# Strided heads: the products with the values issued four quarters in turn

## The chip, the cores and the metric

One core of a Trainium2 chip runs the whole program. The metric is device microseconds (us) of one execution. TensorE (PE, with its weight loads shown as PEld) does the matrix products, VectorE (DVE) and ScalarE (ACT) the element-wise work, SyncE (SP) issues most transfers, and GpSimd (POOL) does almost nothing here.

## The reference

An attention over 4 batches, 8 heads, 576 positions and head size 64 is followed by two gated feed-forward blocks (model size 512, inner size 1024). Four heads are local (each position looks back over 32 positions), four are strided:

```python
mask_strided = (rel >= 0) & (pos[None, :] % stride == pos[:, None] % stride)
...
scores = np.where(masks[None, :, :, :], scores, -1000000000.0)
scores = scores - np.max(scores, axis=-1, keepdims=True)
attn = np.exp(scores)
attn = attn / (np.sum(attn, axis=-1, keepdims=True) + 1e-09)
return np.matmul(attn, v).astype(np.float32)
```

In a strided head only positions of one residue modulo 32 see each other, so the 576 positions fall into 32 classes of 18. The change touches only the last product of these heads, attention weights by values.

## The kernel before, in words

**Strided heads.** The kernel sorts positions by residue and takes three residues together: a block of 3 x 18 = 54 positions (SQ), 11 blocks a head. A pair of heads (ab = 0 and 1) of one batch is handled in two halves of 6 and 5 blocks (SB): one call of `unit` (lines 422 to 580) each, 16 such units in all (4 batches, 2 pairs, 2 halves). A unit makes the scores (line 467), masks them with a maximum on DVE (line 483), takes exponentials on ACT (line 488), normalises on DVE (line 499), turns two blocks at a time on PE (line 522) and copies the result into the tile `pt` (turned_out, lines 527 to 533). Even blocks then lie in rows 0 to 53 of `pt`, odd blocks in rows 64 to 117; the values `vt` lie in the same rows.

**The values' products.** `values` (lines 540 to 553) multiplies, for each block and each of the two heads, 54 rows of values by 54 rows of turned weights. The rows choose the upper or lower half of PE's array and the head the left or right half, so every product occupies one quarter of the array: an even block the two upper quarters, an odd block the two lower ones. Even blocks write the PSUM bank `pv`, odd blocks the bank `tr` in which the turned weights had stood. Each float32 product appears in the trace as two weight loads and two matmuls ("passes"), all on one line, so a unit of 6 blocks has 24 passes and one of 5 blocks 20. Before the change the kernel issues all even blocks, then all odd ones. `place` (lines 561 to 578) copies both banks to the tile xT.

**The strided scores** (line 467) have the same form, 64 rows by 64 columns with 54 columns moving, and the loop there goes over blocks so that four products in a row fall on four different quarters.

**What sets the order.** Everything up to the second feed-forward block is put into a planner (class Plan, lines 73 to 226) as jobs with estimated costs per engine; it lists them by the time at which they can start and by rank, and the instructions are issued on each engine in that order. The cost of a values job stands in line 555; other costs are fixed numbers as well, and PE's change between quarter and whole-array work is counted as 0.09. Up to 60 us of planned time the kernel also issues idle bf16 matmuls (`stir`, line 816) into PE gaps that the plan foresees (lines 863 to 868). Products of the first feed-forward block (line 649, `products`) fill PE between attention jobs. The second block (lines 907 and 975) has a plan of its own.

Of the kernel before, what the change touches and what calls it, by code (L numbers as in the profile page):

```python
# [23 lines left out]
SQ, SR, SB = 3 * NI, 118, (6, 5)  # L24
# [205 lines left out]
def block_kernel(ctx, tc, qkL, qkS, vL, vS, mu_k, mu_r, w_k, w_v, w_r, w_in, conv_w, w_out, ident, mask_l, mask_s, out):  # L230
# [29 lines left out]
    plan = Plan()  # L260
    fixed = {}

    def space(pool_, name, shape, dtype=F32, tag=None, bufs=1, parts=1):
        tag = tag or name
        return Space(tag, bufs, lambda: (pool_() if callable(pool_) else pool_).tile(shape, dtype, name=name, tag=tag, bufs=bufs), parts)
# [156 lines left out]
    def unit(b, p, half, loaded):  # L422

        qk, vts = loaded
        vt = vts[half]
        local = p < 2
        nb, nq, nk, rows = (LB[half], LQ, LK, P) if local else (SB[half], SQ, SQ, SR)
# [11 lines left out]
        n0 = (nb + 1) // 2  # L439
# [19 lines left out]
        pt = space(at, "pt", [P, LB[0] * P], bufs=2, parts=2)  # L459
# [78 lines left out]
        outs_ = [out_] if local else [out_, turned]  # L538

        def values(e):  # L540
            if local:
                for j in range(nb):
                    for ab in range(2):
                        r, o = slice(64 * ab, 64 * ab + 64), pos[j] * P + 64 * (ab ^ turn_of[j])
                        pe.matmul(out_()[r, j * nq:(j + 1) * nq], vt()[:nk, j, r], pt()[:nk, o:o + nq], start=True, stop=True)  # L545
                return

            for odd in range(2):
                rows = slice(64 * odd, 64 * odd + SQ)
                for i in range((nb - odd + 1) // 2):  # L550
                    for ab in range(2):
                        r, o = slice(64 * ab, 64 * ab + 64), i * SR + 64 * (ab ^ (odd and turn_of[1]))
                        pe.matmul(outs_[odd]()[r, i * nq:(i + 1) * nq], vt()[rows, 3 * half + i, r], pt()[rows, o:o + nq], start=True, stop=True)  # L553

        plan.add({"PE": nb * (0.146 if local else 0.105)}, values, [vt, pt], outs_)
        x, n = xT[b], nb * nq
        if local:
            copy(lambda: x()[:, p, 1 + first * nq:1 + (first + nb) * nq], lambda: out_()[:, :n], n, [out_], [(x, 2 * p + half)])
# [23 lines left out]
    def attention(b):  # L582
        xT[b] = space(wx, f"xT{b}", [P, KT, S + 1], tag="xT", bufs=2, parts=9)
        plan.add({"POOL": 0.1}, lambda e: pool.memset(xT[b]()[:, :, 0:1], 0.0), [], [(xT[b], 8)])
        for p in range(4):
            loaded = load(b, p)
            if b == 0 and p == 0:
                consts()
            for half in range(2):
                unit(b, p, half, loaded)  # L590
# [193 lines left out]
    for c in range(2, NCH):  # L784
# [17 lines left out]
        for m in (0, 2, 1, 3):  # L802
            group_v(c, m)
            if c >= 3 and later and (m % 2 or len(later) <= NF):
                f, i = later.pop()
# [75 lines left out]
    plan = Plan()  # L881
# [212 lines left out]
```

## Time and profile before

| | us |
|---|---|
| three runs, median (lowest to highest) | 530.18 (526.58 to 530.76) |
| the profiled execution, its own time | 528.08 |
| its span, first to last instruction | 526.3 |
| PE busy | 513.8 (98%) |
| DVE busy | 387.6 (74%) |
| ACT busy | 365.8 (70%) |
| passes of line 553 into `pv`, busy | 9.1 (192 passes) |
| passes of line 553 into `tr`, busy | 8.3 (160 passes) |

Busy time of PE counts a matmul from its start to its modelled end, and passes on different quarters overlap, so spacing of starts says more than busy time. The attention of the first batch lies in the first 35 us, that of the others in three stretches near 87 to 113, 168 to 197 and 244 to 268 us. The granted TensorE clock is full but for one stretch near 28 us.

### The profile page before, as it was taken

How to read it: one execution, taken by the hardware profiler on the slowest of the kernel's cores; microseconds unless marked ns; L12 is line 12 of the kernel's file. 1: busy time of each engine (PE TensorE's matmuls, PEld its weight loads, DVE VectorE, ACT ScalarE, POOL GpSimd, SP SyncE). 2: the span in 40 equal slices, each digit the busy share in tenths (PEclk: the TensorE clock that was granted, in tenths of full speed). 3: DMA queues.
4: the chain of work that ended last, by engine and by line, in shares of the span. 5: the costliest groups of instructions: out<-in, count | busy, mean ns of one | idle time of the engine just before them, and what ended most of it. 6: DMA issues, size and time to landing. Idle time of an engine off the chain costs nothing.

```text
span 526.3 us, 12014 instructions
## 1 busy us (share of the span) xinstructions
PE 513.8 (98%) x4470; PEld 476.7 (91%) x4470; DVE 387.6 (74%) x1125; ACT 365.8 (70%) x1086; POOL 1.6 (0%) x15
## 2 busy tenths in 40 slices
PE   7899999999999999999999999999999999999997
PEld 4679999899999899999999999989898989999885
DVE  4989999999956998955777414499996576677620
ACT  5999996999758999667989354475764454455420
POOL 0000000000000000000000000000000000000000
PEclk9989999999999999999999999999999999999999
DMA  7974566977566892771374440745127015401011
GB/s 221 337 236 151 168 195 200 369 233 245 190 209 211 284 352 100 258 272 50 122 254 185 139 141 1 284 148 203 41 72 283 22 40 181 176 20 41 20 42 60
DMA packets 50122, 88.87 MB, mean 169 GB/s; under 512 B 4240, under 2 KB 32528, under 8 KB 50064
## 3 DMA queue, kind: packets, MB, share of 16 engines
q1 hardware_dynamic: 49776, 87.95, 49.6%
q8 instruction: 35, 0.57, 0.5%
q14 instruction: 23, 0.19, 0.1%
q10 hardware_dynamic: 288, 0.16, 0.1%
HBM read 59.46 MB, written 28.64 MB: 167 GB/s over the span
## 4 chain that ended last, share of the span: by engine, by line
PE 75%; ACT 13%; DMA 5%; DVE 5%; issue 1%; ACTq 0%; DVEq 0%; SPq 0%
PE mm L649 37%; PE oo L975 18%; PE hh L907 14%; ACT pr L488 3%; ACT wb L299 2%; PE sc L467 2%; DMA x<-x_d 1%; DMA wi_d<-ws 1%; PE pv L545 1%; ACT mx L628 1%; PE pv L553 1%; DMA raw<-in_w_k 1%; DVE pr L483 1%; PE tr L522 1%; ACT rl L672 1%
## 5 line engine op out<-in xcount | busy, mean ns | idle before, releaser
L907 PEld LDWEIGHTS hh<-x,wi 128*128 128x128 f32 x672 | 94.8, 188 | 6.6 <-DVE hb L919 2.0
L907 PE MATMUL hh<-x,wi 128*128 128x288 f32 x672 | 98.5, 296 | 1.2 <-DVE hb L919 1.0
L649 PE MATMUL mm<-X,wvh 128*128 128x288 f32 x448 | 86.5, 301 | 0.0
L649 PEld LDWEIGHTS mm<-X,wvh 128*128 128x128 f32 x448 | 67.1, 188 | 1.0
L649 PE MATMUL mm<-Y,wkh 128*128 128x288 f32 x384 | 67.4, 294 | 0.0
L488 ACT ACTIVATE pr<-pr,nmx 128x54 f32<-128x54 f32 (+1 forms) x160 | 55.5, 358 | 5.8 <-DVE nmx L483 5.8
L649 PEld LDWEIGHTS mm<-Y,wkh 128*128 128x128 f32 x384 | 56.3, 188 | 0.1
L649 PE MATMUL mm<-Y,wrh 128*128 128x288 f32 x256 | 54.9, 302 | 0.5 <-ACT rs L661 0.5
L954 DVE SCALAR_TENSOR_TENSOR c<-hb,cw_sb,c 128x576 f32<-128x576 f32 x64 | 50.6, 812 | 0.0
L649 PE MATMUL mm<-X,wvl 128*128 128x288 f32 x224 | 47.9, 295 | 0.0
L690 DVE TENSOR_TENSOR X<-sq,X 128x288 fp32r<-128x288 f32 x48 | 21.9, 457 | 30.4 <-ACT X L688 24.6
L649 PEld LDWEIGHTS mm<-Y,wrh 128*128 128x128 f32 x256 | 42.4, 191 | 1.5 <-ACT rs L661 0.8
L975 PE MATMUL oo<-wo,gAh 128*128 128x512 f32 x160 | 43.4, 393 | 0.0
L649 PE MATMUL mm<-Y,wkl 128*128 128x288 f32 x192 | 40.9, 294 | 0.0
L649 PE MATMUL mm<-Y,wrl 128*128 128x288 f32 x128 | 38.3, 299 | 0.2 <-DVE wrl L350 0.2
L649 PEld LDWEIGHTS mm<-X,wvl 128*128 128x128 f32 x224 | 35.9, 188 | 0.0
L975 PE MATMUL oo<-wo,gBh 128*128 128x512 f32 x128 | 34.5, 392 | 0.0
L488 ACT ACTIVATION_READ_ACCUMULATOR pr<-pr,nmx 128x1 f32 x160 | 32.5, 203 | 0.0
L672 ACT ACTIVATE rl<-mm 128x288 f32<-128x288 f32 x64 | 26.6, 416 | 7.8 <-PE mm L649 7.6
L975 PEld LDWEIGHTS oo<-wo,gAh 128*128 128x128 f32 x160 | 28.1, 188 | 3.8
L649 PEld LDWEIGHTS mm<-Y,wkl 128*128 128x128 f32 x192 | 30.6, 188 | 0.0
L925 ACT ACTIVATE hb<-hb 128x288 f32<-128x288 f32 (+1 forms) x32 | 18.0, 564 | 15.4 <-DVE hb L919 15.3
(114 smaller groups left out, 1059.9 us busy)
## 6 DMA issues: line engine op xcount, KB each, us to landing
x_d<-xo SPq DMA_DIRECT2D x42, 288.0 KB, 3.9
x<-x_d SPq DMA_DIRECT2D x21, 576.0 KB, 4.9
wi_d<-ws SPq DMA_DIRECT2D x24, 256.0 KB, 4.3
wi<-wi_d SPq DMA_DIRECT2D x6, 896.0 KB, 6.3
qk<-in_qkS SPq DMA_DIRECT2D x8, 599.0 KB, 5.4
out<-ob SPq DMA_DIRECT2D x18, 256.0 KB, 2.0
qk<-in_qkL SPq DMA_DIRECT2D x7, 592.0 KB, 5.8
raw<-in_w_k SPq DMA_DIRECT2D x8, 512.0 KB, 3.7
```

Of the source, the lines that this page charges most:

```text
L299: act.activation(b(), hw, AF.Copy, scale=REBIAS)
L467: pe.matmul(bank_of[j]()[to:to + 64, at_[j]:at_[j] + nk], qk()[r, qo[j]:qo[j] + LQ], qk()[r, ko[j]:ko[j] + nk], start=True, stop=True)
L483: dve.tensor_tensor_reduce(pr()[:, i * gap:i * gap + nk], bank_of[i]()[:, at_[i]:at_[i] + nk], masks[i], -1.0 / 8.0, 3.0e38, ALU.add, ALU. ...
L488: act.activation(pr()[:, k], pr()[:, k], AF.Exp, bias=nmx()[:, i:i + 1], scale=-1.0, accum_out=sums()[:, i:i + 1])
L522: pe.transpose(turned()[:n, i // 2 * SR:(i // 2 + 1) * SR], pr()[:SR, i * gap:i * gap + n], id_sb[:SR, :SR])
L649: pe.matmul(o(), w_cols(name, j, t, part), x_[t](), start=(t == 0 and part == 0 and x_ is xhi), stop=(t == nk - 1 and x_ is xlo))
L672: plan.add({"ACT": 0.295}, lambda e: act.activation(r(), o(), AF.Relu), [o], [r])
L690: plan.add({"DVE": 0.37}, lambda e: dve.tensor_tensor(l_(), sq(), h_().bitcast(F32), ALU.subtract), [sq, h_], [l_])
L907: pe.matmul(o(), w(hw, j), x()[:, hx, j], start=anew and n == 0 and j == 0, stop=last and n == 2 and j == 1, skip_group_check=True)
L925: act.activation(h()[:, cols], h()[:, cols], AF.Relu)
L954: plan.add({"DVE": 0.735}, lambda e, k=k: dve.scalar_tensor_tensor(c(), h()[:, k:k + S], cw_sb[:, k * NF + f:k * NF + f + 1], c(), ALU.mul ...
L975: pe.matmul(o(), x_()[:, f, col:col + P], wsp["wo", f]()[:, part], start=(f == 0 and x_ is th and part == 0), stop=(f == NF - 1 and x_ is tl))
```

## The change

Inside `values`, the loop over pairs of blocks goes outside and the loop over even and odd inside, so that the products of one even and one odd block come one after the other. Operands, banks and the number of instructions are the same. The planner's cost of a strided values job goes from 0.105 to 0.07 for each block.

```diff
-            for odd in range(2):
-                rows = slice(64 * odd, 64 * odd + SQ)
-                for i in range((nb - odd + 1) // 2):
+            for i in range(n0):
+                for odd in range(min(2, nb - 2 * i)):
+                    rows = slice(64 * odd, 64 * odd + SQ)
                     for ab in range(2):
                         r, o = slice(64 * ab, 64 * ab + 64), i * SR + 64 * (ab ^ (odd and turn_of[1]))
                         pe.matmul(outs_[odd]()[r, i * nq:(i + 1) * nq], vt()[rows, 3 * half + i, r], pt()[rows, o:o + nq], start=True, stop=True)
 
-        plan.add({"PE": nb * (0.146 if local else 0.105)}, values, [vt, pt], outs_)
+        plan.add({"PE": nb * (0.146 if local else 0.07)}, values, [vt, pt], outs_)
```

## Rows read from the trace of the kernel before

**Rows 1.** Windows by stage: stretch, length, busy time (instructions) per engine, clock, DMA.

```profile
core 0: us, PE busy (x) PEld busy (x) DVE busy (x) ACT busy (x) POOL busy (x), PEclk, DMA share, GB/s
...
22.00:35.00 13.00, 11.53 (x182) 9.07 (x180) 11.67 (x51) 12.40 (x47) 0.00 (x0) 0.87 0.88 255
...
87.00:105.30 18.30, 17.96 (x306) 16.03 (x305) 17.25 (x95) 17.09 (x76) 0.00 (x0) 1.00 1.00 333
105.30:162.00 56.70, 56.67 (x515) 55.57 (x516) 46.70 (x137) 46.96 (x148) 0.10 (x1) 1.00 0.66 218
...
173.00:268.00 95.00, 95.00 (x1102) 90.47 (x1100) 75.01 (x284) 80.81 (x289) 0.00 (x0) 1.00 0.59 203
```

**Rows 2.** Waits of PE, 100 to 340 us: total us, times, longest.

```profile
PE pv L545 <- ACT xT L284: 1.0, 1, 1.0
PE pv L553 <- ACT xT L576: 0.4, 1, 0.4
```

**Rows 3.** Chain that ended last, near 28 us: start, us, what.

```profile
27.93 0.38 PE pv L553 x6
...
31.38 0.36 PE pv L553 x6
```

**Rows 4.** Line 553 over the span: ns min/median/max, first and last start.

```profile
L553 PE MATMUL pv<-pt,vt x192: 210/218/311, 23.2 to 267.7; 54*64 54x54 f32 x192
...
L553 PE MATMUL tr<-pt,vt x160: 218/218/348, 23.3 to 267.8; 54*64 54x54 f32 x160
```

**Rows 5.** PE's timeline, a 6-block values unit: start, us, instructions.

```profile
264.67 0.38 PE L553 MATMUL pv<-pt,vt 54*64 54x54 f32 x6
264.84 0.27 PE L553 MATMUL tr<-pt,vt 54*64 54x54 f32 x2
...
265.05 0.34 PE L553 MATMUL tr<-pt,vt 54*64 54x54 f32 x6
```

**Rows 6.** PE's timeline, a 5-block values unit and the product behind it.

```profile
267.38 0.38 PE L553 MATMUL pv<-pt,vt 54*64 54x54 f32 x6
...
267.76 0.22 PE L553 MATMUL tr<-pt,vt 54*64 54x54 f32 x2
267.92 0.40 PE L649 MATMUL mm<-Y,wrh 128*128 128x288 f32 x1
```

**Rows 7.** PE's timeline, strided scores of 6 and of 5 blocks.

```profile
247.13 0.57 PE L467 MATMUL sc<-qk 64*64 64x54 f32 x24
...
250.15 0.56 PE L467 MATMUL sc<-qk 64*64 64x54 f32 x20
```

**Rows 8.** PE's timeline, a 6-block values unit with local scores behind it.

```profile
188.56 0.38 PE L553 MATMUL pv<-pt,vt 54*64 54x54 f32 x6
...
189.12 0.51 PE L467 MATMUL sc<-qk 64*64 64x96 f32 x13
189.55 0.40 PE L649 MATMUL mm<-X,wvh 128*128 128x288 f32 x1
```

**Rows 9.** PE's timeline, local scores of 4 blocks between whole-array products.

```profile
244.19 0.56 PE L467 MATMUL sc<-qk 64*64 64x96 f32 x16
244.69 0.40 PE L649 MATMUL mm<-X,wvh 128*128 128x288 f32 x1
```

**Rows 10.** Windows around the low clock, columns as in rows 1.

```profile
24.80:28.20 3.40, 2.24 (x43) 1.44 (x42) 3.40 (x11) 3.40 (x13) 0.00 (x0) 0.98 1.01 280
28.20:31.60 3.40, 3.40 (x39) 3.02 (x41) 2.82 (x13) 3.17 (x13) 0.00 (x0) 0.52 0.57 162
```

**Rows 11.** PE's timeline, neighbouring products at the low and the full clock.

```profile
30.70 0.44 PE L649 MATMUL mm<-Y,wrl 128*128 128x288 f32 x1
30.94 0.44 PE L649 MATMUL mm<-Y,wrh 128*128 128x288 f32 x1
...
35.72 0.29 PE L649 MATMUL mm<-Y,wrl 128*128 128x288 f32 x1
35.85 0.43 PE L649 MATMUL mm<-Y,wrh 128*128 128x288 f32 x2
```

## The prediction

> **What bounds the kernel now.** I began with the windows by stage, because the average share of PE hides which stretches are its own. From 173 to 268 us PE is busy for all of the 95.00 us, and from 105.3 to 162 us for 56.67 of 56.70, at the full clock [rows 1]. There a shorter piece of PE work shortens the program. Earlier this doesn't hold: from 22 to 35 us ACT is busy for 12.40 of 13.00 us and PE for 11.53, and from 87 to 105.3 us PE still has gaps while DVE and ACT are above 17 of 18.3 us [rows 1]. Next I read the waits. After 100 us PE's attention jobs stood still twice in all: a local values job waited 1.0 us for ACT's copy to xT, and a strided values job 0.4 us for the copy of the unit before it, both for the single `pv` bank [rows 2]. The chain of waits then says which early values jobs matter: those that begin at 27.9 and 31.3 us are on it [rows 3]. Last I took the timeline of PE at single units, since the passes of line 553 last 0.218 us each but overlap [rows 4]; only first start, last end and the neighbours tell what a unit occupies.
>
> **What a values unit costs now.** A 6-block unit goes from 264.67 to 265.05 + 0.34 = 265.39: 0.72 us (rounding aside, 0.73). Its odd passes, in the bank `tr`, do not wait for the last even one: the first starts at 264.84, 0.17 us in, and from there the four quarters run together; but at the end six `tr` passes stand alone, with the upper half of the array empty [rows 5]. So PE already overtakes in part what the order of issue keeps apart, and only the rest can be won. A 5-block unit goes from 267.38 to 267.76 + 0.22, or 0.60 us (two more passes start a little later in that last row) [rows 6].
>
> **What it costs afterwards.** The nearest row is a close one: the strided scores run 64-column weights and 54 moving columns, with four quarters in turn, and take 0.57 us for 24 passes and 0.56 us for 20 [rows 7]. The 5-block unit has hardly less, since the two upper quarters still have six passes each, and the deepest quarter sets the end. Passes last 0.218 us in both. So a 6-block unit saves 0.73 - 0.57 = 0.16 us and a 5-block unit 0.60 - 0.56 = 0.04, which with the rounding I take as 0.05. The one difference is the order of the quarters: neighbours in the scores' order share no half, those in the new values' order share the upper or the lower one. But the even passes before the change, two quarters of one half, already run side by side [rows 5], so I expect no cost from it.
>
> A rule speaks against this. 23 steps between 24 starts take 0.57 - 0.22 = 0.35 us in the scores, about 15 ns a step [rows 4, 7]. The Trainium skill, "TensorE: Matmul & The Clock Gate", section "Wait — 56ns, not 53.3ns?", says that start-to-start never drops below about 25 ns however small the matmul is. An estimate by that page would be 23 x 25 = 575 ns, more than the 0.51 us between first and last start of today's unit, and so no gain at all. The trace disagrees for passes on different quarters, with 15 ns.
>
> **Where the values are followed by scores.** At 188.56 us the unit is followed by 16 passes of local scores, and they already fill the empty upper half: from the unit's start to the next whole-array product is 189.55 - 188.56 = 0.99 us [rows 8]. The same 16 passes alone take 244.69 - 244.19 = 0.50 [rows 9]. In the new order they can enter after 0.35 us plus one step of a quarter (six passes in 0.35, so about 0.06), which gives 0.91 us and saves 0.08; the upper bound is the whole 0.16. I take 0.10, nearer to the lower end because the cover is visible.
>
> **The sum.** Eight units have 6 blocks and eight have 5: 192 + 160 = 352 = 8 x 24 + 8 x 20 passes [rows 4]. Eleven start at 105.3 us or later, in stretches where PE sets the pace [rows 1].
> - Two 6-block units without scores behind them: 2 x 0.16 = 0.32.
> - Three 6-block units with scores behind them: 3 x 0.10 = 0.30.
> - Six 5-block units: 6 x 0.05 = 0.30.
> - The five early units (four in the first batch, one just ahead of the 0.4 us wait): 0 if ACT and DVE hide them all, 3 x 0.16 + 2 x 0.05 = 0.58 at most. The one ahead of the wait is hidden, since ACT is late there [rows 2]; two are on the chain [rows 3], 0.16 + 0.05. I take 0.2.
>
> That is 1.1 us, with 0 and 8 x 0.21 = 1.7 as bounds. Nothing is added: the number of instructions, transfers and banks is the same. No wait is new, since odd products write the bank `tr` only after turned_out has read it, and every values product needs turned_out's result anyway. `place` reads even blocks first; their last pass is late by one or two steps of 15 ns, the odd ones are early by 0.16. That copy is on ACT's or DVE's queue, with others ahead of it, and I count it as nothing.
>
> **The planner's cost** is the second half of the change, and its price can't be read from any row. The plan now counts 5 x 0.07 + 0.09 = 0.44 us for a 5-block unit, against 0.35 + 0.16 = 0.50 by rows (last start, then the step to the next product, [rows 6, 7]); before it was 5 x 0.105 + 0.09 = 0.62 against 0.54 from first pass to next product [rows 6]. Both are off by less than 0.1, so the plan isn't misled by much. But its later choices between jobs that are ready at nearly one time can flip from 23 us on. I bound this by what such choices cost today: the waits of 1.0 and 0.4 us could vanish or come again [rows 2], and so could the stretch at 28 us in which the granted clock is 0.52, the level of 1.2 GHz [rows 10]. There products start 0.24 us apart, against 0.13 at 2.4 GHz [rows 11]; in 3.4 us that loses 3.4 x (1 - 0.13 / 0.24) = 1.6 us of PE work. So about -3.0 to +3.0 us around the sum, and I take zero as the value, having no reason for a sign.
>
> **Against which time.** The profiled execution took 528.08 us (span 526.3 and 1.8 around it), so by its own time I get 527.0. It lies 2.1 below the median of the three runs, 530.18. Four executions are known, 526.58 to 530.76; the middle of them is (528.08 + 530.18) / 2 = 529.1, and 529.1 - 1.1 = 528.0 is my forecast. About 1%, 5.3 us, is what a measurement of this kernel can tell from no change, and the forecast lies well inside.
>
> **Rivals.**
> - **The order does nothing.** PE already runs odd passes ahead of the last even ones [rows 5]; if pairs in one half of the array hold each other up, two by two, the new order gives what the old one gave. For: the shared half is the one thing that the scores' rows don't have. Against: even passes of one half already start together. Time 529.1. The page's least step of 25 ns would end in the same time. Chance 0.10.
> - **Slower: the plan opens a new hole early.** Its place is the first 35 us, where PE has gaps and idle matmuls fill only those that the plan foresees. Before the low clock PE was busy for 2.24 of 3.40 us [rows 10]; a shorter values unit leaves it less busy still, and a second such stretch, on the path, costs 1.6. From one on it outweighs the 1.1: 529.1 - 1.1 + 1.6 = 529.6; with a new wait of 1.0 at the `pv` bank, 530.6. Against: the low stretch lies where ACT is nearly full, so part of it is hidden. Chance 0.22; over 1% needs four or five such events, 0.08.
> - **Faster by more: the new order closes the holes.** Without the two waits and the low stretch: 529.1 - 1.1 - 1.4 - 1.6 = 525.0. For: each of them hangs on a few tenths of a us of order. Against: the two later stretches have no hole to close. Chance 0.15.
> - The forecast itself has 0.53.
>
> **Range and chances.** The forecast's own range, with its bounds of 0 and 1.7 us and the spread of the known executions (2.1 to each side), is 525.5 to 530.5. With the two rivals on either side it reaches from 524.0 to 532.0, and leaves out about 2 in 10. Faster by over 1% (0.09) comes from the third rival with a low draw of runs, slower by over 1% (0.08) from the second; 0.83 is left for within 1%.
>
> **What would show it.** In the changed kernel's timeline a 6-block unit alternates two `pv` and two `tr` passes from the start, and lasts 0.57 us from first start to last end; a 5-block unit lasts 0.56. With scores behind it, first pass to next product falls from 0.99 to about 0.9. If units still last 0.72, the first rival holds. The windows from 105.3 us on should be shorter by 0.9 in all with PE as full as before. A second stretch at the low clock, or new lines among the waits of PE of 0.4 us or more, would show the planner's part to be larger than the products' own; then the forecast is wrong by that part, whichever way it goes.

## The result, and the profile after

The changed kernel takes 524.72 us (median of 6 runs, 523.68 to 525.66) against 529.38 us before in the same comparison (6 runs, 526.58 to 530.76): ratio 0.9916, 95% interval 0.9888 to 0.9944. It is faster by 4.7 us, some four times what was forecast, and inside the stated range. The profiled execution took 523.68 us with a span of 521.9, where before had 528.08 and 526.3.

The units themselves first: the windows of line 553 alone, around a 6-block unit and a 5-block unit of the changed kernel (stretch, length, PE busy with its number of passes, weight loads, clock, transfers).

```profile
261.60:262.40 0.80, 0.57 (x24) 0.44 (x24) 1.00 0.00 0
263.80:264.50 0.70, 0.56 (x20) 0.43 (x20) 1.00 1.07 369
```

0.57 us stands where the timeline before gave 0.72 [rows 5], and 0.56 where it gave 0.60 [rows 6]: both numbers of the strided scores [rows 7], to the hundredth. PE's timeline of the changed kernel shows how: `pv` and `tr` passes take turns two by two from the start, and none stands alone at the end.

```profile
261.68 0.27 PE L553 MATMUL pv<-pt,vt 54*64 54x54 f32 x2
261.69 0.27 PE L553 MATMUL tr<-pt,vt 54*64 54x54 f32 x2
...
262.01 0.22 PE L553 MATMUL pv<-pt,vt 54*64 54x54 f32 x2
262.02 0.23 PE L553 MATMUL tr<-pt,vt 54*64 54x54 f32 x2
```

Now the stages of the changed kernel, columns as in [rows 1]:

```profile
22.00:35.00 13.00, 11.52 (x177) 8.95 (x174) 12.79 (x39) 12.81 (x42) 0.00 (x0) 1.00 0.95 258
...
87.00:105.30 18.30, 18.23 (x327) 16.51 (x326) 17.29 (x103) 18.20 (x82) 0.00 (x0) 1.00 1.02 342
105.30:162.00 56.70, 56.41 (x501) 55.60 (x492) 43.95 (x121) 46.08 (x143) 0.11 (x1) 1.00 0.60 199
...
173.00:268.00 95.00, 94.51 (x1090) 90.28 (x1083) 77.36 (x279) 81.87 (x295) 0.00 (x0) 1.00 0.65 220
```

Nearly everything is earlier than before, so the stretches do not hold the same work, and their busy times can't be compared one by one. PE is not quite as full in the two late ones: it has gaps of 0.29 and 0.49 us, where before had 0.03 and none [rows 1]. The clock from 22 to 35 us is full, where it was 0.87 [rows 1, 10]. PE's waits between 100 and 340 us, which were 1.0 and 0.4 us [rows 2], are now 0.4 and 0.3 us. The longer one is gone, that of line 553 has stayed, and one is new:

```profile
PE sc L467 <- DVE nmx L483: 0.4, 1, 0.4
PE pv L553 <- ACT xT L576: 0.3, 1, 0.3
```

So the units shrink as was forecast, and yet by the forecast's sum that is worth 1.1 us and not 4.7. The planner's cost is the other half of the change, and the two had to be taken apart.

### The profile page after: what moved, and what is told of

Its sections match the earlier page's. It is cut to its first block, busy times and chain, and to the rows that moved or that the text cites. A ratio compares the mean times of both kernels' runs of the same rounds, so it can differ in the third digit from the quotient of the medians.

```text
span 521.9 us, 12036 instructions
## 1 busy us (share of the span) xinstructions
PE 511.6 (98%) x4474; PEld 474.3 (91%) x4474; DVE 388.0 (74%) x1123; ACT 364.6 (70%) x1088; POOL 1.6 (0%) x15
## 4 chain that ended last, share of the span: by engine, by line
PE 73%; ACT 11%; DVE 8%; DMA 5%; issue 1%; POOL 0%; DVEq 0%; ACTq 0%; POOLq 0%
PE mm L649 35%; PE oo L975 19%; PE hh L907 15%; ACT pr L488 3%; DMA raw<-in_w_r 2%; DMA wi_d<-ws 2%; ACT wb L299 2%; DVE pr L483 1%; PE sc L467 1%; DMA raw<-in_w_v 1%; DMA raw<-in_w_k 1%; ACT mx L628 1%; DVE wt L310 1%; DVE c L954 1%; PE tr L511 1%
```

## Experiments

### One half of the change at a time

The old cost with the new loop leaves every other instruction in the order of before; the new cost with the old loop has the order of the changed kernel.

```diff
 # e1: the new loop, and
-        plan.add({"PE": nb * (0.146 if local else 0.07)}, values, [vt, pt], outs_)
+        plan.add({"PE": nb * (0.146 if local else 0.105)}, values, [vt, pt], outs_)
 # e2: the old loop, and
-        plan.add({"PE": nb * (0.146 if local else 0.105)}, values, [vt, pt], outs_)
+        plan.add({"PE": nb * (0.146 if local else 0.07)}, values, [vt, pt], outs_)
```

Expected of e1: 

> The new loop with the planner's old cost of 0.105: the order of all other instructions is that of before. Products theory (the quarters give the whole gain): about 524.7 as in the changed kernel, 4 to 5 us under before. Plan theory (the products give what the units' own times say, the rest comes from the planner's new order): a 6-block unit lasts 0.57 us and a 5-block unit 0.56, and the time falls by 0.9 to 1.7 us only, ratio 0.997 to 0.998.

Expected of e2: 

> The old loop with the planner's new cost of 0.07: all other instructions stand as in the changed kernel. Products theory: no change from before, within 1 us. Plan theory: 2.5 to 3.5 us under before (the measured 4.5 less 0.9 to 1.7), with the units lasting 0.73 and 0.61 us as before.

Expected of the changed kernel once more: 

> The changed kernel once more, on the chip and beside the runs that the next two share, so that the four corners (loop old or new, cost old or new) are all measured with many runs: 524.0 to 525.5, ratio 0.991 to 0.995. If the products and the plan add up, it lies 0.5 to 1.5 us under the old loop with the new cost (525.2).

| loop | cost | us, median (runs) | before beside it (runs) | ratio, 95% interval |
|---|---|---|---|---|
| new | 0.105 (e1) | 527.90 (12) | 528.08 (32) | 0.9988 [0.9967, 1.0009] |
| old | 0.07 (e2) | 525.17 (9) | 528.08 (32) | 0.9945 [0.9922, 0.9969] |
| new | 0.07 (first) | 524.72 (6) | 529.38 (6) | 0.9916 [0.9888, 0.9944] |
| new | 0.07 (again) | 525.40 (6) | 529.31 (17) | 0.9923 [0.9901, 0.9946] |

The runs of before differ between the rows (528.08 to 529.38 us), so rows are compared by their ratios. The products theory falls: the new loop alone moves the time by -0.1%, with an interval of -1.7 to +0.5 us that holds the forecast of 1.1 but can't be told from nothing; the ratio of 0.997 to 0.998 that was expected of e1 was missed. The planner's cost alone gives -0.55%, 2.9 us, as expected of e2, whose units last 0.73 and 0.61 us in its trace, as before. On top of it the new loop seems to bring another 0.2 to 0.3%, about 1.2 to 1.5 us by the two rows at the bottom. The intervals overlap, so the times alone don't show this part. The second measurement was expected 0.5 to 1.5 us under e2; by ratio it is, but its 525.40 us are not less than e2's 525.17.

**Where the plan's gain lies.** e1 and the changed kernel have the same products and differ in the plan alone, and neither profiled execution has a stretch at the low clock before the end. Their pages, span and PE's busy time, e1 first:

```profile
span 525.4 us, 12012 instructions
...
PE 511.6 (97%) x4470; PEld 474.0 (90%) x4470; DVE 387.6 (74%) x1125; ACT 365.4 (70%) x1086; POOL 1.6 (0%) x15
```

```profile
span 521.9 us, 12036 instructions
...
PE 511.6 (98%) x4474; PEld 474.3 (91%) x4474; DVE 388.0 (74%) x1123; ACT 364.6 (70%) x1088; POOL 1.6 (0%) x15
```

PE is busy for 511.6 us in both. What remains of the span, 13.8 against 10.3 us, is PE's idle time, and its difference of 3.5 us is the whole difference of the spans. By windows, 1.4 us of it lie before 87 us, 1.5 from 87 to 173 us and 0.7 from 300 to 380 us. The plan doesn't make PE's work shorter; it closes holes. These are single executions. Two others of the same two plans and the new loop point the same way: PE is idle for 15.3 us in e12 (the old cost, below) and for 12.0 in the second profile of the changed kernel.

One hole shows how. PE's wait of 1.0 us for ACT's copy to xT [rows 2] is at 172 us, and it is there in e1 too (0.94 us). ACT's timeline before, with PE's values job behind it:

```profile
168.80 0.80 PE L545 MATMUL pv<-pt,vt 96*64 96x64 f32 x20
...
170.43 0.34 ACT L488 ACTIVATE pr<-pr,nmx 128x54 f32<-128x54 f32 x1 [0.88 <-DVE nmx L483]
...
172.39 0.42 ACT L284 ACTIVATE xT<-pv 128x320 f32<-128x320 f32 x1
...
172.86 0.69 PE L545 MATMUL pv<-pt,vt 96*64 96x64 f32 x16 [0.98 <-ACT xT L284]
```

The copy that frees the bank `pv` stands in ACT's queue behind the next unit's exponentials; these wait for DVE, and so the copy comes 2.8 us after the values (168.80 + 0.80) that it reads. In the changed kernel the plan has put the same copy ahead of those exponentials:

```profile
166.44 0.80 PE L545 MATMUL pv<-pt,vt 96*64 96x64 f32 x20
...
167.38 0.42 ACT L284 ACTIVATE xT<-pv 128x320 f32<-128x320 f32 x1
...
168.65 0.34 ACT L488 ACTIVATE pr<-pr,nmx 128x54 f32<-128x54 f32 x1
...
169.81 0.69 PE L545 MATMUL pv<-pt,vt 96*64 96x64 f32 x16
```

The copy now follows its values job by a tenth of a us, and PE doesn't wait. This hole goes with the plan: in the profiles with the old cost for the later batches it is 0.98 us (before), 0.94 (e1), 1.06 (e10), 0.63 (e12) and 0.51 (e7), and in those with the new cost, the changed kernel twice, e2 and e8, there is none. (e4, with 0.05, has none either, but one of 1.6 us at line 467 near 169 us, and it gains as much.) The same kind of wait early on, for the copy of a strided unit, is 0.93 us in e1 and 0.30 after (PE's timelines):

```profile
24.93 0.27 PE L553 MATMUL pv<-pt,vt 54*64 54x54 f32 x2 [0.93 <-ACT xT L576]
```

```profile
24.51 0.27 PE L553 MATMUL pv<-pt,vt 54*64 54x54 f32 x2 [0.30 <-ACT xT L576]
```

**Why e1 doesn't show all of its products' gain.** In its third late stretch, where PE has no hole, it does: from the local scores at the start (before [rows 9]) to the product behind the last values unit before took 267.92 - 244.19 = 23.73 us [rows 6, 9], and in e1's timeline it takes 266.46 - 243.21 = 23.25:

```profile
243.21 0.56 PE L467 MATMUL sc<-qk 64*64 64x96 f32 x16
...
266.46 0.40 PE L649 MATMUL mm<-Y,wrh 128*128 128x288 f32 x1
```

That is 0.48 us for two units of each kind, 2 x 0.16 + 2 x 0.05 = 0.42 by the sum. Elsewhere e1 waits more than before. These waits of PE from 100 to 380 us are not in the profile of before, which has in that stretch only the two of [rows 2] and the 1.0 us at line 907 that before, e1 and the changed kernel all have:

```profile
PE hh L907 <- DMA x<-x_d: 0.7, 1, 0.7
...
PE mm L649 <- ACT rs L661: 0.4, 1, 0.4
```

PE's busy time falls from 513.8 to 511.6 us, of which the low clock of that one execution of before accounts for up to 1.6, and idle time rises from 12.5 to 13.8. A PE that is ahead sooner can wait for the others sooner; that these waits come from this was not tested, though the 0.7 us at line 907 stands again in e12, which has the same plan and units of the same length. The runs of before spread over 6.0 us (525.67 to 531.65 of 32), and what moves them wasn't settled; the section on the low clock has what the record shows of it.

### Is a lower cost better because it is truer?

```diff
-        plan.add({"PE": nb * (0.146 if local else 0.07)}, values, [vt, pt], outs_)
+        plan.add({"PE": nb * (0.146 if local else 0.0875)}, values, [vt, pt], outs_)   # e3; 0.05 in e4
```

Expected of e3: 

> The new loop with a planner's cost of 0.0875, midway: another order of the other instructions. Plan theory in the form that the new order is a lucky draw: anything from 523 to 530, not between e1 and the changed kernel by need. Plan theory in the form that a lower cost is truer and so better: about 526, between e1 (528.0) and the changed kernel (524.7). Products theory: 524.7.

Expected of e4: 

> The new loop with a planner's cost of 0.05, below what the units last. Lucky draw: anything from 523 to 530. Truer-is-better: worse than the changed kernel, about 526, since the cost is now too low. Products theory: 524.7.

e3, midway between the costs, gains nothing: 527.88 us, ratio 1.0002 [0.9979, 1.0024]. e4, too low, gains as much as the changed cost within the intervals: 525.13 us, 0.9952 [0.9924, 0.9981]. Counting the switch of 0.09, a 5-block unit from its first pass to the next product lasts 0.49 us by the changed kernel's timeline, while 0.0875 says 0.53, 0.07 says 0.44 and 0.05 says 0.34:

```profile
263.83 0.27 PE L553 MATMUL pv<-pt,vt 54*64 54x54 f32 x2
...
264.32 0.40 PE L649 MATMUL mm<-Y,wrh 128*128 128x288 f32 x1
```

The two that are low by 0.05 and 0.15 gain, the one that is high by 0.04 doesn't. So nearness to the truth doesn't order them. A lucky draw of another order fits all four costs, but so does a rule that nobody tried: the two costs that count too much (0.105 and 0.0875) gain nothing, while the other two both gain, and equally within their intervals. These runs can't tell the two apart.

### Which part of the plan?

```diff
+        plan.add({"PE": nb * (0.146 if local else 0.07 if b == 0 else 0.105)}, values, [vt, pt], outs_)   # e7
+        plan.add({"PE": nb * (0.146 if local else 0.105 if b == 0 else 0.07)}, values, [vt, pt], outs_)   # e8
```

Expected of e7: 

> The new loop, planner's cost 0.07 for the first batch alone and 0.105 for the others: the order up to about 85 us is that of the changed kernel. If the plan's 2.8 us (cost alone against before) come from the start (fewer gaps before 30 us, fewer stretches at the low clock), about 525.5. If they come from the later stretches (fewer changes between quarter and whole-array work), about 527.5, near the 527.9 of the new loop with the old cost.

Expected of e8: 

> The mirror image: planner's cost 0.105 for the first batch and 0.07 for the others; the order up to about 85 us is that of before. If the start gives the plan's gain, about 527.5; if the later stretches do, about 525.5. If both give some, both kernels lie near 526.5.

e7 takes 525.21 us, 0.9948 [0.9927, 0.9969]; e8 525.81 us, 0.9966 [0.9948, 0.9983], both beside before at 527.64 (19 runs). Against e1's 0.9988, which has the same loop, the early cost gains 0.4% and the late one 0.2%, the whole 0.65 to 0.72%. Both parts seem to give some, and within their intervals they add up. The early part's gain is nearly clear of noise, since the intervals of e7 and e1 overlap by only 0.0002; the late part's is not, with an overlap of 0.0016 between e8 and e1. The times don't lie near 526.5, as was expected if both give some, but 0.7 and 1.3 us below. The profiles are on the side of both: before 87 us PE is idle for 5.0 us in e7, against 6.2 in e8 and 6.1 in e1; from 87 to 300 us for 1.4 in e7 and 0.9 in e8, against 2.3 in e1.

### The low clock

Of the runs with the early order of before, 4 of 12 (e1) and 8 of 12 (e8) had a granted clock of 0.997 or less over the whole span, and so had 24 of the 68 of the kernel before beside e1 to e12; with the new early order it was 0 of 12 in the changed kernel (both times), 0 of 8 in e7 and 1 of 9 in e2. So the new early order nearly does away with the low clock. Whether that gains anything was tried with more idle matmuls in the early gaps:

```diff
-                            stir(n, bank(), anew)
+                            stir(n + 4, bank(), anew)
```

Expected of e10 (on e1): 

> The new loop with the old cost (e1, 527.9) and four more idle matmuls in every early PE gap that the plan sees (all other instructions in the same order). If the old plan's early gaps bring the low clock and the low clock costs time: no run at the low clock (4 of 12 before) and 526.5 to 527. If the low clock is hidden by ACT and DVE: no run at the low clock, but 527.5 to 528. If the idle matmuls delay work: over 528.5.

Expected of e11 (on the changed kernel): 

> The changed kernel with four more idle matmuls in every early gap. The new plan shows no low clock early, so nothing is to be gained by theory: 524.3 to 525.3, as without them; over 525.5 if the idle matmuls delay the first products.

In e10 none of 12 runs is below 0.999, and the time is 529.34 us beside 529.31 before, ratio 1.0003 [0.9986, 1.0021]; e1 had 0.9988. By its time alone e10 falls under its third expectation, over 528.5, but before took as long beside it. e11 gives 525.44, 0.9935 [0.9914, 0.9956]. So more idle matmuls gain nothing. Either the low stretch lies under ACT, as [rows 1] suggest, or the idle matmuls cost what it does; and e10 differs in more than the clock, since its profile has 2.4 us of idle PE between 173 and 300 us, where e1's has 0.4.

The other runs don't agree on what the low clock costs. In e8 the eight runs at the lower clock and the four others have the same median, 525.8 us, and in e1 the two medians are 0.4 us apart. But among the runs of before those at 0.997 or less are slower by 2.2 us (12 of the 32 beside e1 to e4), 1.4 (6 of 19, beside e5 to e8) and 0.7 (6 of 17, beside e9 to e12), and in e3 by 2.9 (4 of 12). That the clock itself costs this isn't shown: in e3's profile it is low from 100 to 105 us (0.66), right behind a stop of PE of 2.4 us at line 467. For the plan's gain it matters little. Counting only runs at 0.998 or more, e2 takes 525.15 us (8 runs) against 527.54 before (20), which keeps 2.4 of the 2.9 us; e1, at 527.83 (8), is then not ahead of before at all.

### The products by themselves, four times over

```diff
 # e5: the old loop
-                for i in range((nb - odd + 1) // 2):
+                for i in list(range((nb - odd + 1) // 2)) * 4:
 # e6: the new loop
-            for i in range(n0):
+            for i in list(range(n0)) * 4:
```

Expected of e5: 

> The old loop, planner's cost 0.105, each of its two halves run four times over (the same result is written again), so that what the order costs is four times as large. Theory of a short lead (PE lets odd passes start only about three passes of a quarter, 0.17 us, ahead of the end of the even ones): a 6-block unit runs its even passes for 24 x 0.058 = 1.40 us, the first odd one starts at about 1.23, the last ends at about 2.85. Theory of free overtaking (the old loop's odd passes fill in wherever quarters are free): about 1.65, as with the new loop. Theory of a least step of 25 ns per pass whatever the quarter: 96 x 25 ns, 2.4 us and more.

Expected of e6: 

> The new loop, planner's cost 0.105, run four times over. Short lead and free overtaking alike: four quarters together for 24 passes deep, 1.40 + 0.23, about 1.63 us a 6-block unit. Least step of 25 ns: 2.4 us and more, as with the old loop. The time against the old loop four times over: 9 to 15 us less by the short lead (5 x 1.2 + 6 x 0.75 in the stretches that PE sets, up to 15.6 for all sixteen units), about 0 by the two others.

The windows of line 553 over one 6-block unit, e5 and then e6:

```profile
118.06:120.90 2.84, 2.82 (x96) 2.69 (x96) 1.00 0.67 233
```

```profile
112.28:113.90 1.62, 1.62 (x96) 1.49 (x96) 1.00 0.96 308
```

2.82 and 1.62 us, for 2.85 and 1.63 expected: short lead, and no free overtaking. The least step of about 25 ns between starts that the Trainium skill states ("TensorE: Matmul & The Clock Gate", section "Wait — 56ns, not 53.3ns?") would by an estimate, 96 x 25 ns, need 2.4 us in e6 too. The trace disagrees for passes on different quarters, with 96 passes in 1.62 us. The first odd passes of e5's unit in its timeline:

```profile
118.06 1.43 PE L553 MATMUL pv<-pt,vt 54*64 54x54 f32 x42
119.28 0.27 PE L553 MATMUL tr<-pt,vt 54*64 54x54 f32 x2
```

42 of 48 even passes have started when the first odd one does, 6 are left. In the unit before the change it was 6 of 12, 6 left again [rows 5]. So PE's lead is not a share of the unit but a fixed number of passes, or the time that these take; the two lengths can't tell which.

The times are 567.56 us (2 runs; 1.075 [1.0701, 1.0799]) and 552.63 us (2 runs; 1.0467 [1.0419, 1.0515]), 14.9 us apart. They are no clean measure, since PE also stood still inside some of these units (below) and the granted clock over the span was 0.98 and 0.99.

### The order of the quarters

```diff
-                for odd in range(min(2, nb - 2 * i)):
-                    rows = slice(64 * odd, 64 * odd + SQ)
-                    for ab in range(2):
+                for odd, ab in ((0, 0), (1, 1), (1, 0), (0, 1)):
+                    rows = slice(64 * odd, 64 * odd + SQ)
+                    if odd < nb - 2 * i:
```

Expected of e12: 

> The new loop with the planner's old cost, and the four products of a pair of blocks in the order of the scores, in which neighbours share no half of the array. If neighbours in one half held each other up, units would last less than 0.57 and 0.56 us; if not, as I expect, the same 0.57 and 0.56.

The windows of line 553 in e12, 6 and 5 blocks:

```profile
264.70:265.50 0.80, 0.57 (x24) 0.44 (x24) 1.00 0.81 281
267.30:268.10 0.80, 0.57 (x20) 0.44 (x20) 1.00 0.10 20
```

0.57 us as in the changed kernel, and the 5-block unit 0.01 longer. So neighbours in one half of the array don't hold each other up in these products. (Its one run took 528.57 us, with the old cost.)

## Why the prediction was right, and where it was not

**The number** came inside the stated range, but mostly not for the forecast's reason. The forecast's own range, 525.5 to 530.5 us, doesn't hold 524.72; the wider one holds it by 0.7 us, because it had been drawn out to take in the rivals. The larger part of the 4.7 us, 2.9 by e2, is a term that the forecast had put at zero.

**The unit's cost** was right in each term: 0.57 and 0.56 us, from the one row that had the same form with four quarters in turn. The reason given, that PE overtakes in part and only the rest can be won, is shown by e5 and e6.

**Values with scores behind them** were put at a gain of 0.10 between 0.08 and 0.16. In e1's timeline such a unit goes from 187.22 to the product at 188.06, 0.84 us against 0.99 [rows 8], a gain of 0.15:

```profile
187.22 0.27 PE L553 MATMUL pv<-pt,vt 54*64 54x54 f32 x2
...
187.61 0.52 PE L467 MATMUL sc<-qk 64*64 64x96 f32 x16
188.06 0.40 PE L649 MATMUL mm<-X,wvh 128*128 128x288 f32 x1
```

The lower end was too careful. It let the scores enter at 0.41 us and take 0.50 us up to the next product; here they enter at 0.39 and take 0.45.

**The sum of the products**, 1.1 us, is shown in its units but not as a whole. It lies in e1's interval (1.7 to -0.5), which holds nothing as well, and near the 1.2 to 1.5 that the loop seems to add to the new plan. Its 0.9 us in the late stretches needs a PE without holes; the third stretch gave 0.48 for 0.42, and e1's profile has new waits elsewhere that are as long as the rest.

**The planner's cost** is the step that failed: "I take zero as the value, having no reason for a sign". It measured -2.9 us (e2), at the edge of the bounds of -3.0 to +3.0. The rival "the new order closes the holes" (525.0 us, chance 0.15) names what happened, down to the 1.0 us wait at `pv`. That the bounds just hold the value is partly luck. They were rightly built from the holes of the trace, but 1.6 of their 3.0 us was the low clock, of which at most about 0.5 shows in the plan's gain, and they were too small in the number of holes: they counted two waits after 100 us, where PE's idle time is 12.5 us in all, 6.3 of it in the first 87 us by the windows of before, and none of that was in my sum. For the sign I still see no reason in the profile: with the same loop, neighbouring costs give 0 (e3) or -2.5 us (e4); whether costs that don't count too much gain as a rule stays open.

**The first rival** (the order does nothing) falls by the units' rows. **The slower rival** had a true half: e1's profile has new waits of 0.7 and 0.4 us, with the plan of before.

**What the profile was to show** came true for the units; "a second stretch at the low clock, or new lines among the waits of PE" was the test for the plan's part, and it looked only for harm. Waits that vanish are the same evidence with the other sign.

## What to carry to other kernels

When a change also touches a number that a scheduler plans by, cost it as two changes: the old number with the new code keeps the order of everything else and shows what the code is worth. List every hole of the bounding engine, early ones too, and take their sum as the most that a new order can win; what it can lose is not in that list. Issue products on different quarters in turn, since here PE ran only 6 passes ahead of the order of issue; count the passes of the deepest quarter to see what is left to win.

## What was not expected of the hardware

PE's lead over the order of issue is 6 passes in both lengths tried ([rows 5] and e5), so in a unit of 12 even passes the odd ones began about halfway through them.

In the kernels with four times the products, PE stopped inside values units with nothing in the profile to wait for. The waits of e6 and its instruction transfers:

```profile
PE pv L553 <- issue: 6.0, 3, 3.2
```

```profile
q8 instruction: 43, 0.70, 0.5%
```

Three stops make 6.0 us, the longest 3.2; the queue that carries instructions moved 43 packets where before it moved 35 (0.57 MB). In the same view of the kernel before line 553 has no such wait. That late instructions are the cause is a guess; it wasn't tried. The larger number of instructions can't be all of it, for stops of the same kind stand at line 467, near 96 us, in kernels without the fourfold products, whose queue moved 35 packets: 1.2 us in the second profile of the changed kernel, 1.4 in e2 and 2.4 in e3. The first two in PE's waits:

```profile
PE sc L467 <- issue: 1.2, 1, 1.2
PE sc L467 <- issue: 1.4, 1, 1.4
```

The first profile of the changed kernel has none, so the same program has such a stop in one execution and not in another. That can be a part of what moves its time.
